# Products over 40 head dims and of 40 output rows, issued with the two head parities in turns

## The chip, the cores and the metric

The kernel runs on one core of a Trainium2 chip. The metric is the device time of one execution in microseconds. TensorE does the products, VectorE (DVE in the profile) and ScalarE (ACT) read its results from PSUM, GpSimd (POOL) does two elementwise products and the indirect DMAs, SyncE issues most DMAs.

## What is computed

Two blocks follow each other, all in float32. The first is a recurrence over 768 time steps for 4 batch rows and 8 heads of 40 dims:

```python
for t in range(S):
    kt, vt, rt = (k[:, :, t], v[:, :, t], r[:, :, t])
    wt, at, bt = (w[:, :, t], a[:, :, t], b[:, :, t])
    y[:, :, t] = np.einsum('bhd,bhde->bhe', rt, state)
    Sa = np.einsum('bhde,bhe->bhd', state, at)
    state_decay = state * wt[:, :, None, :] - np.einsum('bhd,bhe->bhde', Sa, bt)
    state = state_decay + np.einsum('bhd,bhe->bhde', vt, kt)
```

Its output, 3072 rows of 8 x 40 = 320, goes through a layer of 8 experts: each row takes the expert with the largest logit, `relu(x @ w1[e]) @ w2[e]` with 1024 hidden columns, times that expert's softmax weight.

## The kernel before

The first part cuts the time into 6 chunks of 128 steps. A unit `u` is one chunk `c` of one batch row `b`, with all 8 heads: 24 units, the batch rows going fastest. Heads come in pairs: head 2p + par lies at partitions par x 64 to par x 64 + 39 of a tile, for p from 0 to 3 (`rows(par)`); par is the head's parity. A product over the 40 head dims therefore uses rows 0 to 63 of TensorE's array for parity 0 and rows 64 to 127 for parity 1. One with 40 output rows uses one half of its columns in the same way.

For each unit `prepare` forms the running product of the decay, scales the inputs and transposes four of them (`ps_nat`, L169). `systems` builds, for one parity and then the other, four masked products over the 40 dims of both operands, 128 x 128 for each of the four heads: GT, NT0, N and AT (L177, mask on VectorE at L182). From NT0 and N it forms powers: NT1 and the next N, to NT5, each a product of 128 x 128 matrices, copied by ScalarE (L180). `attend` then, parity by parity, forms the right side r (a product with the state, 40 rows, L224, and one with GT, 128 rows, L225, into one bank), and runs X through eight steps (`ps_q`, L216): each is a product of one NT with X and a sum on VectorE (L233, L242), and the next needs that sum. The result u is transposed (`ps_uT`, L246). Then for each parity: ZT, a masked product over 40 dims (L177 again); y, of three products for each head (with the state S, 40 rows, L263; with AT, L264; with ZT, L267); the state's update `ps_s` of 40 output rows (L273, L274), and the transpose of the new state (`ps_st`, L284). `route` transposes the rows of y, forms the logits and stores the rows.

PSUM's eight banks are shared by two kinds of tiles: `big` has five, `small` three, each tile in a bank of its own.

The second part ranks the rows by expert, gathers them and runs the expert layers (L474, L487).

The kernel is written in the order above, with `prepare` and `systems` of the next unit ahead of `attend`, but the instructions of each engine are put in order by a scheduler when the program is built. It moves work of the next unit's `systems` between the dependent steps of X. The order shown below is what it made.

## Time and profile before

| | |
|---|---|
| median of 2 runs | 2519.51 us (2518.1 to 2520.93) |
| profiled execution, first to last instruction | 2515.5 us |
| PE busy | 2373.8 us |
| PEld (weight loads) busy | 2069.5 us |
| DVE, ACT, POOL busy | 529.6, 415.7, 151.8 us |
| mean granted TensorE clock | 0.716 of full speed |

The profiled execution is 4.0 us shorter than the median, for what lies around the instructions. The clock has two levels, full (2.4 GHz, 1.0 in the profile) and half (1.2 GHz, 0.5); a mean between them is a mix of stretches. A float32 product appears as two weight loads (PEld) and two matmuls (PE) for each head; a transpose as one of each. A steady unit stands between 868 and 960 us; most rows below are from it.

### The profile page before, as it was taken

How to read it: one execution, taken by the hardware profiler on the slowest of the kernel's cores; microseconds unless marked ns; L12 is line 12 of the kernel's file. 1: busy time of each engine (PE TensorE's matmuls, PEld its weight loads, DVE VectorE, ACT ScalarE, POOL GpSimd, SP SyncE). 2: the span in 40 equal slices, each digit the busy share in tenths (PEclk: the TensorE clock that was granted, in tenths of full speed). 3: DMA queues.
4: the chain of work that ended last, by engine and by line, in shares of the span. 5: the costliest groups of instructions: out<-in, count | busy, mean ns of one | idle time of the engine just before them, and what ended most of it. 6: DMA issues, size and time to landing. Idle time of an engine off the chain costs nothing.

```text
span 2515.5 us, 29177 instructions
## 1 busy us (share of the span) xinstructions
PE 2373.8 (94%) x12916; PEld 2069.5 (82%) x12916; DVE 529.6 (21%) x1157; ACT 415.7 (17%) x849; POOL 151.8 (6%) x185
## 2 busy tenths in 40 slices
PE   6999999999999999999999999999999998699998
PEld 5999988998898898898899899899889887244544
DVE  2212222122122122122212112213112111311110
ACT  1312211221121121121121121111112110001010
POOL 4000000000000000000000000000000000311101
PEclk9877657766765766666676676676677665799999
DMA  1000000000000000000000000000000000522210
GB/s 48 19 9 11 19 19 16 4 19 19 1 19 19 3 17 19 10 10 19 16 3 19 16 4 19 19 1 19 19 1 19 3 1 3 155 93 85 86 51 16
DMA packets 20560, 59.58 MB, mean 24 GB/s; under 512 B 2893, under 2 KB 14159, under 8 KB 18512
## 3 DMA queue, kind: packets, MB, share of 16 engines
q1 hardware_dynamic: 16992, 48.50, 6.6%
q0 software_dynamic: 3072, 9.18, 1.2%
q8 instruction: 102, 1.67, 0.3%
q14 instruction: 26, 0.21, 0.0%
q10 hardware_dynamic: 368, 0.01, 0.0%
HBM read 49.82 MB, written 9.18 MB: 23 GB/s over the span
## 4 chain that ended last, share of the span: by engine, by line
PE 82%; issue 11%; DVE 3%; POOL 2%; ACT 1%; DMA 0%; POOLq 0%; DVEq 0%; ACTq 0%
PE ps_q L216 20%; PE ps_NT L177 14%; PE ps_N L177 11%; PE ps_y L264 4%; PE ps_ZT L177 4%; PE ps_y L267 4%; PE ps_y L263 3%; PE ps_nat L169 3%; PE ps_r L225 3%; PE ps_r L224 3%; PE ps_AT L177 3%; PE ps_GT L177 3%; DVE X L233 2%; POOL out_dram L493 1%; PE ps_st L284 1%
## 5 line engine op out<-in xcount | busy, mean ns | idle before, releaser
L216 PE MATMUL ps_q<-X,NT 128*128 128x40 f32 x2304 | 399.7, 332 | 52.7 <-DVE X L233 50.2
L216 PEld LDWEIGHTS ps_q<-X,NT 128*128 128x128 f32 x2304 | 378.2, 248 | 70.1 <-DVE X L233 65.7
L177 PE MATMUL ps_NT<-NT,N 128*128 128x128 f32 x1920 | 332.6, 326 | 1.3 <-ACT N L180 1.0
L177 PEld LDWEIGHTS ps_NT<-NT,N 128*128 128x128 f32 x1920 | 282.6, 226 | 13.2 <-issue 8.9
L177 PE MATMUL ps_N<-N,NT 128*128 128x128 f32 x1536 | 249.7, 317 | 0.0
L180 ACT COPY NT<-ps_NT 128x512 f32<-128x512 f32 x240 | 140.4, 585 | 584.9 <-PE ps_NT L177 584.9
L177 PEld LDWEIGHTS ps_N<-N,NT 128*128 128x128 f32 x1536 | 235.2, 234 | 0.0
L233 DVE TENSOR_TENSOR X<-ps_q,X 128x160 f32<-128x160 f32 x240 | 77.6, 323 | 574.9 <-PE ps_q L216 574.9
L474 PE MATMUL hp<-xgT,w 128*128 128x512 f32 (+1 forms) x384 | 190.9, 627 | 0.0
L474 PEld LDWEIGHTS hp<-xgT,w 128*128 128x128 f32 (+1 forms) x384 | 63.2, 189 | 122.4 <-issue 120.4
L216 PE MATMUL ps_q<-Z,NT 128*128 128x40 f32 x768 | 142.1, 348 | 20.5 <-DVE Z L242 20.5
L216 PEld LDWEIGHTS ps_q<-Z,NT 128*128 128x128 f32 x768 | 135.8, 266 | 27.7 <-DVE Z L242 27.7
L487 PE MATMUL zp<-w,h_sb 128*128 128x320 f32 x512 | 145.0, 433 | 0.0
L180 ACT COPY N<-ps_N 128x512 f32<-128x512 f32 x192 | 112.3, 585 | 107.9 <-PE ps_N L177 107.9
L264 PE MATMUL ps_y<-natK,AT 128*128 128x40 f32 x384 | 123.0, 420 | 0.0
L487 PEld LDWEIGHTS zp<-w,h_sb 128*128 128x128 f32 x512 | 94.6, 191 | 34.5 <-issue 0.8
L267 PE MATMUL ps_y<-natB,ZT 128*128 128x40 f32 x384 | 120.1, 415 | 0.0
L267 PEld LDWEIGHTS ps_y<-natB,ZT 128*128 128x128 f32 x384 | 101.9, 327 | 6.8 <-issue 4.3
L264 PEld LDWEIGHTS ps_y<-natK,AT 128*128 128x128 f32 x384 | 96.4, 311 | 13.3 <-issue 0.9
L177 PE MATMUL ps_ZT<-in,uT 40*128 40x128 f32 x384 | 101.0, 440 | 4.6 <-ACT uT L248 2.7
L263 PE MATMUL ps_y<-S,in 40*128 40x40 f32 x320 | 100.9, 414 | 0.0
L158 POOL MEMSET PT<- 128x4 f32 x24 | 2.5, 105 | 1573.8 <-DVE ST L279 1280.2
(150 smaller groups left out, 2384.4 us busy)
## 6 DMA issues: line engine op xcount, KB each, us to landing
in<-in_packed_dram SPq DMA_DIRECT2D x48, 480.0 KB
w<-in_moe_w_dram SPq DMA_DIRECT2D x8, 1280.0 KB
w<-in_moe_w_dram SPq DMA_DIRECT2D x8, 1024.0 KB
x_rows<-xs SPq DMA_DIRECT2D x24, 160.0 KB
w<-in_moe_w_dram SPq DMA_DIRECT2D x8, 256.0 KB
xg<-x_rows,g_idx POOLq DMA_INDIRECT x32
out_dram<-zo,s_idx POOLq DMA_INDIRECT x32
wg_sb<-in_moe_w_gate_dram ACTq DMA_DIRECT2D x2, 4.0 KB
```

The lines of the kernel that those rows point to most:

```text
L169: nc.tensor.transpose(ps[:, p, :], src[:, p, :], ident[:])
L177: nc.tensor.matmul(ps[:, p, :], lhsT=lhs(p), rhs=rhs(p), start=True, stop=True)
L180: nc.scalar.copy(t[:], ps[:])
L216: nc.tensor.matmul(q[:, p, :], lhsT=m[:, p, :], rhs=x[:, p, :], start=True, stop=True)
L224: nc.tensor.matmul(q[:, p, :], lhsT=I[rs, A, p, :], rhs=ST[rs, p, :], start=True, stop=False)
L225: nc.tensor.matmul(q[:, p, :], lhsT=d["GT", par][:, p, :], rhs=nV[:, p, par, :D], start=(c == 0), stop=True,)
L233: nc.vector.tensor_tensor(Xn[:], q[:], X[:], op=ALU.add)
L263: nc.tensor.matmul(q[:, p, :], lhsT=I[rs, R, p, :], rhs=Sn[rs, p, :], start=True, stop=False)
L264: nc.tensor.matmul(q[:, p, :], lhsT=d["AT", par][:, p, :], rhs=nK[:, p, par, :D], start=(c == 0), stop=False,)
L267: nc.tensor.matmul(q[:, p, :], lhsT=ZT[:, p, :], rhs=nB[:, p, par, :D], start=False, stop=True)
L474: nc.tensor.matmul(hp[:, :cols], lhsT=g["w"][0][:dsz, db, fb * 128 : (fb + 1) * 128], rhs=g["xT"][:dsz, db, :cols], start=(db == 0), stop= ...
L487: nc.tensor.matmul(zp[:], lhsT=g["h"][:, fb, j * 128 : (j + 1) * 128], rhs=g["w"][1][:, fb, :], start=(fb == 0), stop=(fb == FB - 1),)
```

## The change

Products over the 40 head dims are issued for both parities together: for each p the product of parity 0 and then that of parity 1, each parity into its own bank. That holds for GT, NT0, N, AT and ZT (the new `product2`), for the products with the state in r and y, and for the new state's transposes. The `ps_s` products share one bank and turn between the two column halves. In r, y and `ps_s` all products with the state (or all of the first kind) come first and those over 128 rows after them, so one bank holds several open sums; only the first product into it starts the bank. All r products now stand ahead of both parities' X steps. `product` keeps the 128-row products alone. Comments and the docstring are taken out. Numbers of products, evacuations and DMAs stay.

```diff
@@ -171,36 +171,48 @@
...
-        def product(lhs, rhs, mask, tag, bufs):
+        def product2(lhs, rhs, mask, tag, bufs):
+
+            pss = [big("ps_" + tag) for _ in range(2)]
+            for p in range(NP):
+                for par in range(2):
+                    nc.tensor.matmul(pss[par][:, p, :], lhsT=lhs(par, p), rhs=rhs(par, p), start=True, stop=True)
+            ts = []
+            for par in range(2):
+                t = sb.tile([128, NP, 128], F32, name=tag, bufs=bufs)
+                nc.vector.tensor_tensor(t[:], pss[par][:], mask[:, None, :].to_broadcast([128, NP, 128]), op=ALU.mult)
+                ts.append(t)
+            return ts
+
+        def product(lhs, rhs, tag, bufs):
             ps = big("ps_" + tag)
             for p in range(NP):
-                nc.tensor.matmul(ps[:, p, :], lhsT=lhs(p), rhs=rhs(p), start=True, stop=True)
+                nc.tensor.matmul(ps[:, p, :], lhsT=lhs[:, p, :], rhs=rhs[:, p, :], start=True, stop=True)
             t = sb.tile([128, NP, 128], F32, name=tag, bufs=bufs)
-            if mask is None:
-                nc.scalar.copy(t[:], ps[:])
-            else:
-                nc.vector.tensor_tensor(t[:], ps[:], mask[:, None, :].to_broadcast([128, NP, 128]), op=ALU.mult)
+            nc.scalar.copy(t[:], ps[:])
             return t
...
+
+            def of(n):
+                return lambda par, p: I[rows(par), n, p, :]
+
+            d["GT"] = product2(of(K), of(A), before, "GT", 4)
+            NT0 = product2(of(B_), of(A), before, "NT0", 4)
+            N0 = product2(of(A), of(B_), after, "N", 4)
+            d["AT"] = product2(of(V), of(R), before, "AT", 4)
+            d["NT"] = []
             for par in range(2):
-                def of(n, par=par):
-                    return lambda p: I[rows(par), n, p, :]
-
-                def mat(t):
-                    return lambda p: t[:, p, :]
-                d["GT", par] = product(of(K), of(A), before, "GT", 4)
-                NTk = product(of(B_), of(A), before, "NT0", 4)
-                Nk = product(of(A), of(B_), after, "N", 4)
-                d["AT", par] = product(of(V), of(R), before, "AT", 4)
-                d["NT", par] = [NTk]
+                NTk, Nk = NT0[par], N0[par]
+                chain = [NTk]
                 for i in range(1, LEVELS + 1):
-                    NTn = product(mat(Nk), mat(NTk), None, f"NT{i}", 4)
+                    NTn = product(Nk, NTk, f"NT{i}", 4)
                     if i < LEVELS:
-                        Nk = product(mat(NTk), mat(Nk), None, "N", 4)
+                        Nk = product(NTk, Nk, "N", 4)
                     NTk = NTn
-                    d["NT", par].append(NTk)
+                    chain.append(NTk)
+                d["NT"].append(chain)
...
@@ -216,25 +228,32 @@
...
+            qs = [small("ps_r") for _ in range(2)]
+            if c:
+                for p in range(NP):
+                    for par in range(2):
+                        nc.tensor.matmul(
+                            qs[par][:, p, :], lhsT=I[rows(par), A, p, :], rhs=ST[rows(par), p, :],
+                            start=(p == 0), stop=False, skip_group_check=True,
+                        )
+            for p in range(NP):
+                for par in range(2):
+                    nc.tensor.matmul(
+                        qs[par][:, p, :], lhsT=d["GT"][par][:, p, :], rhs=nV[:, p, par, :D],
+                        start=(c == 0 and p == 0), stop=True, skip_group_check=True,
+                    )
             for par in range(2):
-                rs = rows(par)
-                q = small("ps_r")
-                for p in range(NP):
-                    if c:
-                        nc.tensor.matmul(q[:, p, :], lhsT=I[rs, A, p, :], rhs=ST[rs, p, :], start=True, stop=False)
-                    nc.tensor.matmul(
-                        q[:, p, :], lhsT=d["GT", par][:, p, :], rhs=nV[:, p, par, :D], start=(c == 0), stop=True,
-                    )
+                q = qs[par]
                 X = sb.tile([C, NP, D], F32, name="X", bufs=6)
                 nc.scalar.copy(X[:], q[:])
                 for i in range(LEVELS):
-                    q = apply(d["NT", par][i], X)
+                    q = apply(d["NT"][par][i], X)
...
@@ -252,26 +271,44 @@
...
+            ZT = product2(lambda par, p: uT[rows(par), p, :], lambda par, p: I[rows(par), R, p, :], before, "ZT", 4)
+            qs = [small("ps_y") for _ in range(2)]
+            if c:
+                for p in range(NP):
+                    for par in range(2):
+                        nc.tensor.matmul(
+                            qs[par][:, p, :], lhsT=I[rows(par), R, p, :], rhs=Sn[rows(par), p, :],
+                            start=(p == 0), stop=False, skip_group_check=True,
+                        )
             for par in range(2):
-                rs = rows(par)
-                ZT = product(
-                    lambda p: uT[rs, p, :], lambda p: I[rs, R, p, :], before, "ZT", 2,
-                )
-                q = small("ps_y")
-                for p in range(NP):
-                    if c:
-                        nc.tensor.matmul(q[:, p, :], lhsT=I[rs, R, p, :], rhs=Sn[rs, p, :], start=True, stop=False)
+                for p in range(NP):
                     nc.tensor.matmul(
-                        q[:, p, :], lhsT=d["AT", par][:, p, :], rhs=nK[:, p, par, :D], start=(c == 0), stop=False,
+                        qs[par][:, p, :], lhsT=d["AT"][par][:, p, :], rhs=nK[:, p, par, :D],
+                        start=(c == 0 and p == 0), stop=False, skip_group_check=True,
                     )
-                    nc.tensor.matmul(q[:, p, :], lhsT=ZT[:, p, :], rhs=nB[:, p, par, :D], start=False, stop=True)
-                nc.vector.tensor_tensor(x[:, :, par, :], q[:], nP[:, :, par, :D], op=ALU.mult)
-
-                if c + 1 < NCH:
-                    q = small("ps_s")
-                    for p in range(NP):
-                        nc.tensor.matmul(q[rs, p, :], lhsT=nK[:, p, par, :D], rhs=nV[:, p, par, :D], start=True, stop=False)
-                        nc.tensor.matmul(q[rs, p, :], lhsT=nB[:, p, par, :D], rhs=U[:, p, par, :D], start=False, stop=True)
+                    nc.tensor.matmul(
+                        qs[par][:, p, :], lhsT=ZT[par][:, p, :], rhs=nB[:, p, par, :D],
+                        start=False, stop=True, skip_group_check=True,
+                    )
+                nc.vector.tensor_tensor(x[:, :, par, :], qs[par][:], nP[:, :, par, :D], op=ALU.mult)
+
+            if c + 1 < NCH:
+
+                q = small("ps_s")
+                for p in range(NP):
+                    for par in range(2):
+                        nc.tensor.matmul(
+                            q[rows(par), p, :], lhsT=nK[:, p, par, :D], rhs=nV[:, p, par, :D],
+                            start=(p == 0), stop=False, skip_group_check=True,
+                        )
+                for p in range(NP):
+                    for par in range(2):
+                        nc.tensor.matmul(
+                            q[rows(par), p, :], lhsT=nB[:, p, par, :D], rhs=U[:, p, par, :D],
+                            start=False, stop=True, skip_group_check=True,
+                        )
...
@@ -279,14 +316,17 @@
...
-                    q = small("ps_st")
-                    for p in range(NP):
-                        nc.tensor.matmul(q[rs, p, :], lhsT=STn[rs, p, :], rhs=ident[rs, rs], start=True, stop=True)
-                    nc.scalar.copy(Snn[rs], q[rs])
+                qs = [small("ps_st") for _ in range(2)]
+                for p in range(NP):
+                    for par in range(2):
+                        rs = rows(par)
+                        nc.tensor.matmul(qs[par][rs, p, :], lhsT=STn[rs, p, :], rhs=ident[rs, rs], start=True, stop=True)
+                for par in range(2):
+                    nc.scalar.copy(Snn[rows(par)], qs[par][rows(par)])
```

The scheduler makes another order from it. Three places, on TensorE, for one unit in the middle of the program; the number at a name's end is the buffer, `x4` says that four instructions (one for each p) follow each other.

First, the start of `systems`. Before, `ps_GT_4972` and the three rows after it are parity 0, `ps_GT_5063` and those after it parity 1, 17 rows later:

```order
L177 MATMUL ps_GT_4972<-in2_131 128x128 x4
L177 MATMUL ps_NT0_4979<-in2_131 128x128 x4
L177 MATMUL ps_N_4986<-in2_131 128x128 x4
L177 MATMUL ps_AT_4993<-in2_131 128x128 x4
L177 MATMUL ps_NT1_5000<-NT0_4984,N_4991 128x128 x4
```

```order
L177 MATMUL ps_GT_5063<-in2_131 128x128 x4
L177 MATMUL ps_NT0_5070<-in2_131 128x128 x4
L177 MATMUL ps_N_5077<-in2_131 128x128 x4
L177 MATMUL ps_AT_5084<-in2_131 128x128 x4
L177 MATMUL ps_NT1_5091<-NT0_5075,N_5082 128x128 x4
```

Now (4962 and 4976 are parity 0, 4963 and 4977 parity 1):

```order
L179 MATMUL ps_GT_4962<-in2_131 128x128
L179 MATMUL ps_GT_4963<-in2_131 128x128
L179 MATMUL ps_GT_4962<-in2_131 128x128
L179 MATMUL ps_GT_4963<-in2_131 128x128
L179 MATMUL ps_NT0_4976<-in2_131 128x128
L179 MATMUL ps_NT0_4977<-in2_131 128x128
```

All 32 products of the two parities now stand in one run, in turns, and the powers of both parities follow them.

Second, y. Before, for one parity, the products over 40 rows (L263) stand between those over 128 rows:

```order
L267 MATMUL ps_y_4839<-natB_4035,ZT_4837 128x40
L263 MATMUL ps_y_4839<-S1_2975,in0_129 128x40
L264 MATMUL ps_y_4839<-natK_4028,AT_4070 128x40
L267 MATMUL ps_y_4839<-natB_4035,ZT_4837 128x40
L263 MATMUL ps_y_4839<-S1_2975,in0_129 128x40
```

Now those over 40 rows come first, in turns and ahead of the transposes of u:

```order
L279 MATMUL ps_y_4837<-S1_2970,in0_129 128x40
L279 MATMUL ps_y_4838<-S1_2970,in0_129 128x40
L265 MATMUL ps_uT_4813<-ident_61,u1_145 128x128 x4
L279 MATMUL ps_y_4838<-S1_2970,in0_129 128x40
L285 MATMUL ps_y_4837<-natK_4020,AT_4088 128x40
L285 MATMUL ps_y_4838<-natK_4020,AT_4090 128x40
L300 MATMUL ps_s_4865<-natV_4013,natK_4020 40x40 x8
L306 MATMUL ps_s_4865<-u1_145,natB_4027 40x40
L179 MATMUL ps_ZT_4823<-in0_129,uT_4818 128x128
L179 MATMUL ps_ZT_4824<-in0_129,uT_4818 128x128
```

Behind the ZT products stand seven more of `ps_s`, then the remaining products of y over 128 rows. The next unit's r follows in runs of one parity, not in turns: four of L235, four of L241 (GT), three of L235, one of L235, four of L241.

Third, the end of the X steps. Before:

```order
L177 MATMUL ps_NT5_5147<-NT4_5138,N_5145 128x128 x4
L216 MATMUL ps_q_5231<-X_5229,NT0_4611 128x40 x4
L216 MATMUL ps_q_5238<-X_5236,NT1_4632 128x40 x4
L216 MATMUL ps_q_5245<-X_5243,NT2_4646 128x40 x4
L216 MATMUL ps_q_5252<-X_5250,NT3_4660 128x40 x4
L216 MATMUL ps_q_5259<-X_5257,NT4_4674 128x40 x4
L216 MATMUL ps_q_5266<-X_5264,NT5_4688 128x40 x4
L216 MATMUL ps_q_5273<-Z_5271,NT5_4688 128x40 x4
L216 MATMUL ps_q_5280<-Z_5278,NT5_4688 128x40 x4
```

Now:

```order
L228 MATMUL ps_q_5221<-X_5219,NT0_4525 128x40 x4
L190 MATMUL ps_NT4_5123<-NT3_5114,N_5121 128x128 x4
L190 MATMUL ps_N_5130<-N_5121,NT3_5114 128x128 x4
L228 MATMUL ps_q_5228<-X_5226,NT1_4623 128x40 x4
L190 MATMUL ps_NT5_5137<-NT4_5128,N_5135 128x128 x4
L228 MATMUL ps_q_5235<-X_5233,NT2_4637 128x40 x4
L228 MATMUL ps_q_5242<-X_5240,NT3_4651 128x40 x4
L228 MATMUL ps_q_5249<-X_5247,NT4_4665 128x40 x4
L228 MATMUL ps_q_5256<-X_5254,NT5_4679 128x40 x4
L228 MATMUL ps_q_5263<-Z_5261,NT5_4679 128x40 x4
L228 MATMUL ps_q_5270<-Z_5268,NT5_4679 128x40 x4
```

The second parity's eight steps start earlier: two of them now stand between products of the powers, six stand alone.

Counted over TensorE's order in the first part: places where one product uses another number of array rows or columns than the one ahead go from 1070 to 469, in a full unit from 51 to 23. Places where a product over 40 dims (64 rows of the array) is followed by one in the other row half go from 4 to 1066; turns between the two column halves from 0 to 280.

## Rows read from the trace of the kernel before

**Rows 1.** The page's first part, and the granted clock in 40 slices of its second.

```profile
PE 2373.8 (94%) x12916; PEld 2069.5 (82%) x12916; DVE 529.6 (21%) x1157; ACT 415.7 (17%) x849; POOL 151.8 (6%) x185
...
PEclk9877657766765766666676676676677665799999
```

**Rows 2.** Stretches: start:end, length, busy by engine, PEclk, DMA share, GB/s.

```profile
868.00:960.20 92.20, 89.09 (x512) 83.40 (x510) 19.85 (x42) 15.97 (x33) 2.55 (x3) 0.65 0.05 13
2142.00:2515.00 373.00, 345.07 (x1020) 168.87 (x1020) 59.59 (x169) 32.71 (x64) 67.54 (x68) 0.96 0.26 81
```

**Rows 3.** The chain of waits: start us, us, what; eight loads a row.

```profile
900.18 2.00 PE ps_GT L177 x8
...
905.59 1.71 PE ps_AT L177 x8
...
921.75 0.89 PE ps_NT L177 x8
```

**Rows 4.** Stretches of the unit at 868 us, columns as in rows 2.

```profile
900.18:907.30 7.12, 7.12 (x33) 6.89 (x33) 2.08 (x3) 0.58 (x1) 0.00 (x0) 0.50 0.06 23
920.67:924.90 4.23, 4.23 (x33) 4.01 (x33) 2.08 (x3) 0.58 (x1) 0.00 (x0) 0.87 0.00 0
911.48:916.93 5.45, 5.45 (x49) 5.45 (x50) 0.65 (x2) 2.34 (x4) 0.00 (x0) 1.00 0.01 3
924.90:934.76 9.86, 9.86 (x50) 9.86 (x50) 1.02 (x2) 2.34 (x4) 0.00 (x0) 0.54 0.01 2
...
942.97:958.25 15.28, 12.29 (x65) 11.27 (x64) 2.27 (x7) 0.58 (x1) 0.00 (x0) 0.65 0.00 1
868.11:897.58 29.47, 29.35 (x140) 26.23 (x141) 8.60 (x15) 2.65 (x8) 2.55 (x3) 0.50 0.13 34
```

**Rows 5.** The chain of waits in y and r; two loads a row.

```profile
874.74 0.58 PE ps_y L263 x2
875.31 0.58 PE ps_y L264 x2
875.89 0.43 PE ps_y L267 x2
...
889.98 0.58 PE ps_r L224 x2
...
937.44 0.34 PE ps_r L224 x2
```

**Rows 6.** The chain of waits, ZT of both parities.

```profile
869.83 2.08 PE ps_ZT L177 x8
...
872.59 1.57 PE ps_ZT L177 x6
...
879.48 0.72 PE ps_ZT L177 x2
```

**Rows 7.** The timeline of weight loads at 1885 us: start, us, what, idle before.

```profile
1885.29 2.80 PEld L177 LDWEIGHTS ps_ZT<-in,uT 40*128 40x128 f32 x16 [1.07 <-ACT uT L248]
```

**Rows 8.** Stretches, ZT instructions alone: length, busy PE, PEld, DVE, then PEclk.

```profile
961.90:963.95 2.05, 2.01 (x8) 1.78 (x8) 0.00 (x0) 0.50 0.00 0
...
1885.87:1886.30 0.43, 0.43 (x4) 0.43 (x3) 0.00 (x0) 0.50 0.00 0
1886.30:1886.73 0.43, 0.43 (x6) 0.43 (x6) 0.00 (x0) 0.50 0.00 0
```

**Rows 9.** The chain of waits, two steps of X next to each other.

```profile
951.63 1.94 PE ps_q L216 x8
...
953.97 1.94 PE ps_q L216 x8
```

**Rows 10.** Groups by line on DVE: out, in, count, busy us, mean ns, idle before.

```profile
L161 DVE RECIPROCAL in<-PT 128x512 f32<-128x512 f32 x24 | 80.5, 3352 | 0.8
...
L160 DVE TENSOR_TENSOR_SCAN PT<-in,zeros_c 128x128 f32<-128x128 f32 x96 | 35.1, 409 | 17.0 <-DMA in<-in_packed_dram 15.3
...
L182 DVE TENSOR_TENSOR GT<-ps_GT,before 128x512 f32<-128x512 f32 x48 | 33.2, 692 | 117.0 <-PE ps_GT L177 116.9
```

More of the change, by code (lines that the diff above doesn't have):

```diff
@@ L236, in attend @@
                 for i in range(3):
-                    q = apply(d["NT", par][LEVELS], X)
+                    q = apply(d["NT"][par][LEVELS], X)
                     if i < 2:
@@ L281, in attend @@
                         nc.vector.tensor_tensor(STn[rs], q[rs], PC, op=ALU.mult)
-                    q = small("ps_st")
-                    for p in range(NP):
-                        nc.tensor.matmul(q[rs, p, :], lhsT=STn[rs, p, :], rhs=ident[rs, rs], start=True, stop=True)
-                    nc.scalar.copy(Snn[rs], q[rs])
+                qs = [small("ps_st") for _ in range(2)]
+                for p in range(NP):
+                    for par in range(2):
+                        rs = rows(par)
+                        nc.tensor.matmul(qs[par][rs, p, :], lhsT=STn[rs, p, :], rhs=ident[rs, rs], start=True, stop=True)
+                for par in range(2):
+                    nc.scalar.copy(Snn[rows(par)], qs[par][rows(par)])
             return x
```

## The prediction, made before the changed kernel ran

> **What bounds the kernel.** The page's first and second parts come first [rows 1]: TensorE is busy 94% of the span and its weight loads 82%, while the granted clock stands at 0.5 to 0.8 of full from the second slice to the 35th. The table by stretches then parts the program: a steady unit of the first part takes 92.2 us at a mean clock of 0.65, and the experts take 373 us at 0.96 [rows 2]. The change touches no line of the experts, so these 373 us stay. The chain of waits inside one unit is TensorE almost throughout; the pieces below are read from there.
>
> Three prices follow.
>
> *Weight loads.* Every float32 product is two loads and two matmuls. Eight loads of 128 columns follow each other in 1.71 us at half clock (0.2135 each) and in 0.89 us at full clock (0.111) [rows 3], whether 40 or 128 rows are used: a 40-row product costs what a 128-row one costs.
>
> *Changes of tile.* 40-row operands use half of the array's rows. In the y products each step of 64-row and 128-row tiles shows the cost of going from one to the other: two loads right after a change take 0.58, two without one 0.43 [rows 5]. I take 0.15 us a change at half clock; where the moving side has 128 columns it is 0.29 (2.00 against 1.71 for eight, [rows 3]).
>
> *Two row halves.* In four places of the trace before, all in the last units, the ZT products of one head parity are directly followed by those of the other, in the other half of the rows and another bank. There 16 loads take 2.80 us [rows 7], though eight alone take 1.78 [rows 8], and 16 in one line would need 1.78 + 8 x 0.2135 = 3.49. The cells of 0.43 us show how: three loads touch a cell before the meeting and six at it [rows 8]. The halves work at the same time, each at its own 0.2135. Only some four products on each side meet there; the change makes all of them meet.
>
> **The change, by one full unit.** Each piece is set against the rows of the unit at 868 us.
>
> 1. *GT, NT0, N, AT.* Before: 7.12 + 4.23 = 11.35 us, the first parity at half clock, the second mostly at full [rows 4]. After, the order has all 64 loads in one run, parities in turns. As two lines that is 32 x 0.2135 + 0.29 = 7.1 at half clock. Gain 4.2. Bounds: without any overlap 64 x 0.2135 + 0.29 = 13.95, a loss of 2.6; at full clock VectorE's eight evacuations of 0.692 [rows 10] set at least 5.5, a gain of 5.8. I take half clock, since the stretch ahead of it is at 0.50 [rows 4]. There a pair of products takes 1.71 and its two evacuations 1.38, so VectorE keeps up.
>
> 2. *ZT.* Before 2.08 + 1.57 + 0.72 = 4.37 [rows 6]; after 8 x 0.2135 + 0.37 (the 2.08 less eight loads) = 2.1. Gain 2.3; without overlap 0.6.
>
> 3. *y.* Before, eight times 0.58 + 0.58 + 0.43 = 12.7 [rows 5]. After, 32 loads of 128 rows (6.8), 16 of 64 rows in two lines (1.7), and four changes, since one of the S products lands behind the transposes of u (0.6): 9.1. Gain 3.6; without overlap 1.9.
>
> 4. *r.* Before, eight pieces of 0.58 at half clock and eight of 0.34 at full [rows 5]: 7.4. After, the order has not turned them: four of a parity, then four with GT, and the second parity now comes before the products too, at half clock. 32 loads are 6.8 and six changes 0.9: 7.7. Loss 0.3.
>
> 5. *The clock.* The clock is 1.00 over the six groups at 911.48, falls inside the second parity's products (0.87 on average), and the six groups after them take 9.86 us at 0.54, against 5.45 for the six before [rows 4]. TensorE never paused: it was busy 4.23 of 4.23 us. What differs from the stretches that held full clock is that for these 32 loads only half the array's rows were used. After the change there is no second run of products in the middle, and the one at the start fills both halves. So these six groups run at 5.45: gain 4.4. Bounds: nothing, if the clock falls for another reason; or 1.6 more, if the fuller products raise the clock earlier and two more groups run in 0.89 in place of 1.71 [rows 3].
>
> 6. *The tail of X.* Before, eight groups of q stand at the unit's end with nothing between, 15.28 us [rows 4], each waiting for the sum of the group ahead. With r done early, the order now has two of them between the last N and NT groups; six remain. A group in the tail at half clock is 2.34 us from the next [rows 9], a group between others 5.45 / 6 = 0.91. Gain 2 x 1.43 = 2.9.
>
> Changes of tile in a full unit fall from 51 to 23 by the order. Those outside y, r and ZT change by few, and I take nothing for them. State products (ps_s) in turns use two halves of the columns; no row shows whether these overlap. Their price stays between the present 0.13 for two loads and half of it, under 1.1 us a unit, and I take none.
>
> *What it delays.* Both parities' y now wait for both ZT, so ZT's second evacuation (0.69) stands ahead of the state's sums on VectorE; TensorE has seven state products there (0.9 us) and then the first parity's y. VectorE's scans and the 3.35 us reciprocal [rows 10] for the next unit follow y, and the transposes of K wait for them; between y and these transposes the order has two state transposes, all of r and a group of q, some 11 us against 3.35 + 4 x 0.41 for the scans. If that cover went, the excess would show ahead of K. The second parity's r keeps one of three small banks until its copy; two are left for q, which uses them in turns. No DMA is added or moved past another on SP or POOL. For waits of this kind that I don't see I take off 1 us a unit.
>
> *Sum.* 4.2 + 2.3 + 3.6 - 0.3 + 4.4 + 2.9 = 17.1 a full unit, and 16 of 24 units are full (a state before and after): 274. The first four have no S products and spend less at half clock: ZT, the tail and about 3 of the rest, 8 each, 32. The last four: three with 14, one without a next unit, 6: 48. Together 354, less 24 for waits: 330. The profiled span is 2515.5 and the median of the runs 2519.5, 4 us around the span, which stay: 2519.5 - 330 = about **2190 us**.
>
> **Rivals.**
>
> *A, the clock doesn't follow.* If the fall at 924 us has another cause, piece 5 is gone in some 20 units: 2190 + 88 = 2280. For it: the rise and fall are seen, their cause is inferred from which products stood ahead. Against it: the two falls of this unit come at the half-filled products and in the tail, the two kinds of work that use the array least. The Trainium skill (TensorE: Matmul & The Clock Gate, "HAM oscillation — how this bites in real kernels") puts falls of the clock down to gaps in TensorE's work. The busy 4.23 of 4.23 us does not agree with that; by this rule the change could not move the clock and the time would be A's.
>
> *B, no overlap in strict turns.* The meetings in the trace are between runs of four; single turns may not overlap. Then pieces 1 to 3 lose 6.8 + 1.7 + 1.7 = 10.2 a unit, over 22 units 225: about 2415, still faster through fewer changes, the clock and the tail. Against it: at the meetings, loads of both parities alternate in time already.
>
> *C, full clock earlier.* Fuller products raise the clock during piece 1: 1.4 + 1.6 a unit more, over 20 units 60: 2130. VectorE's 0.692 a product is then the floor, 1.38 against 0.89 for a pair. The Trainium skill (TensorEngine Tiling (Array Packing), "Performance Considerations") says that tiling speeds up TensorE and not the emptying of PSUM; rows 10 agree, and by it C gains no more than this.
>
> *D, slower.* Going from one row half to the other costs like a change of tile, in each of the 1066 places that the order has. At 0.15 to 0.29 each, 0.2 in the middle, 213 us on top of B: about 2630. It decides from 0.10 us a turn (B's 105 us of gain over 1066). Against it: at the four meetings the next load starts within the same cell, with no pause.
>
> That the change doesn't do what it says holds only for r, which the order leaves unturned; that is counted.
>
> **The numbers.** Forecast 0.58, A 0.15, C 0.12, B 0.10, D 0.05. The likeliest is 2190. The range takes in the forecast with its bounds, A and C, and leaves out B and D: 2090 to 2330. A measurement of this kernel can tell about 2% (50 us) from no change. Forecast, A, B and C are all beyond that: faster 0.93; same 0.02 for a case between B and D; slower 0.05.
>
> **What would show it.** Right: 16 loads of GT in some 1.8 to 2.0 us at half clock; one run of products a unit and no half-clock stretch between it and the tail; six q groups in the tail; units of about 75 to 78 us; the experts still 373. Wrong: 16 loads of a pair in 3.4 us or more (B, D); a fall to half clock among the NT and N groups (A); idle TensorE ahead of y, of the transposes of K or among the products, released by VectorE.

## The result, and the profile after

The changed kernel takes 2145.87 us (median of 2 runs, 2145.71 to 2146.03) against 2519.51: a ratio of 0.8495, with a 95% interval of 0.8404 to 0.8586. It is faster by 373.6 us; 330 were predicted (2190, range 2090 to 2330). The profiled execution's span is 2144.2 us (2515.5 before), its mean clock 0.756 (0.716).

The page of the changed kernel, the lines that answer to [rows 1]:

```profile
PE 2009.8 (94%) x12916; PEld 1751.6 (82%) x12916; DVE 511.5 (24%) x1157; ACT 417.3 (19%) x849; POOL 151.1 (7%) x185
...
PEclk9987668756766786678667657866777657999999
```

TensorE is still the bound, with the same number of instructions and the same 94%; it is busy 364 us less. A steady unit, by stretches, answering to [rows 2] (columns as there):

```profile
1148.00:1224.00 76.00, 73.82 (x520) 70.34 (x520) 19.17 (x42) 16.77 (x35) 2.54 (x3) 0.69 0.06 16
```

The chain of waits of the same unit (start us, us, what). It answers to [rows 3, 5, 6]: there, two loads of `ps_y` took 0.58, 0.58 and 0.43 in turn, two of `ps_r` 0.58 at half clock, and ZT took 2.08, 1.57 and 0.72.

```profile
1171.53 1.86 PE ps_y L279 x14
1173.38 1.04 PE ps_uT L265 x4
1174.43 0.58 PE ps_y L279 x2
1175.01 1.00 PE ps_y L285 x4
1176.01 0.69 PE ps_s L300 x16
1176.70 0.12 PE ps_s L306 x2
1176.83 2.06 PE ps_ZT L179 x16
1178.89 0.68 DVE ZT L183
...
1189.17 1.86 PE ps_r L235 x8
1191.03 1.86 PE ps_r L241 x8
1192.88 1.43 PE ps_r L235 x6
...
1194.89 0.58 PE ps_r L235 x2
1195.47 1.86 PE ps_r L241 x8
...
1202.31 2.01 PE ps_GT L179 x16
1204.32 1.71 PE ps_NT L179 x16
1206.02 1.71 PE ps_N L179 x16
1207.73 1.71 PE ps_AT L179 x16
```

What to see: 16 loads of both parities now take what eight loads of one parity took. GT is 2.01 for 16 (2.00 for eight in [rows 3]), AT 1.71 (1.71 for eight). The clock's stretches of this unit and the next:

```profile
1211.80:1239.10 27.30, 26.47 (x231) 26.10 (x229) 3.57 (x11) 10.42 (x19) 0.00 (x0) 1.00 0.00 1
...
1239.10:1286.90 47.80, 46.46 (x284) 43.35 (x283) 15.60 (x31) 5.84 (x15) 2.54 (x3) 0.50 0.09 25
```

There is one stretch at full clock, over the powers and the first q groups of the tail, and one at half clock over the rest. The second half-clock stretch of the kernel before, 924.90 to 934.76 in [rows 4], is gone.

Where the 371.3 us of the span went, cut at the first transposes of u of units 3, 19 and 23:

| stretch | before | after | less | predicted |
|---|---|---|---|---|
| start to unit 3's u | 330.8 | 294.5 | 36.2 | 32 |
| 16 full units | 1460.0 | 1179.9 | 280.1 | 274 |
| last four | 326.8 | 275.3 | 51.5 | 48 |
| behind the last u, with the experts | 397.9 | 394.5 | 3.4 | 0 |
| waits taken off | | | 0 | -24 |

### The profile page after: what moved, and what is told of

Same layout as the page of the kernel before. It is cut to its first block, busy times and chain, and to the rows that moved or that the text cites. A ratio compares the mean times of both kernels' runs of the same rounds, so it can differ in the third digit from the quotient of the medians.

```text
span 2144.2 us, 29192 instructions
## 1 busy us (share of the span) xinstructions
PE 2009.8 (94%) x12916; PEld 1751.6 (82%) x12916; DVE 511.5 (24%) x1157; ACT 417.3 (19%) x849; POOL 151.1 (7%) x185
## 4 chain that ended last, share of the span: by engine, by line
PE 75%; issue 13%; DVE 4%; POOL 2%; DMA 0%; ACT 0%; POOLq 0%; DVEq 0%; ACTq 0%
PE ps_q L228 20%; PE ps_NT L190 11%; PE ps_N L190 8%; PE ps_y L289 4%; PE ps_y L285 4%; PE ps_r L241 4%; PE ps_nat L169 4%; PE ps_r L235 3%; PE ps_y L279 2%; PE ps_ZT L179 2%; PE ps_GT L179 2%; PE ps_AT L179 1%; POOL out_dram L533 1%; PE ps_N L179 1%; DVE X L252 1%
## 5 line engine op out<-in xcount | busy, mean ns | idle before, releaser
L228 PE MATMUL ps_q<-X,NT 128*128 128x40 f32 x2304 | 352.8, 308 | 36.2 <-DVE X L252 36.2
L228 PEld LDWEIGHTS ps_q<-X,NT 128*128 128x128 f32 x2304 | 334.6, 223 | 48.2 <-DVE X L252 47.3
L190 PE MATMUL ps_NT<-NT,N 128*128 128x128 f32 x1920 | 286.5, 297 | 3.9 <-DVE N L183 2.7
L190 PEld LDWEIGHTS ps_NT<-NT,N 128*128 128x128 f32 x1920 | 244.6, 201 | 12.1 <-DVE N L183 5.1
L190 PE MATMUL ps_N<-N,NT 128*128 128x128 f32 x1536 | 212.1, 283 | 0.0
L190 PEld LDWEIGHTS ps_N<-N,NT 128*128 128x128 f32 x1536 | 197.2, 201 | 0.0
L228 PEld LDWEIGHTS ps_q<-Z,NT 128*128 128x128 f32 x768 | 132.2, 260 | 28.7 <-DVE Z L261 28.0
L285 PE MATMUL ps_y<-natK,AT 128*128 128x40 f32 x384 | 115.6, 414 | 0.0
L169 PE MATMUL ps_nat<-ident,in 128*128 128x128 f32 x288 | 71.6, 417 | 24.7 <-DMA in<-in_packed_dram 16.7
L261 DVE TENSOR_TENSOR Z<-ps_q,X 128x160 f32<-128x160 f32 x96 | 31.2, 325 | 225.1 <-PE ps_q L228 225.1
```

What stands on the lines that cost most here:

```text
L169: nc.tensor.transpose(ps[:, p, :], src[:, p, :], ident[:])
L190: nc.tensor.matmul(ps[:, p, :], lhsT=lhs[:, p, :], rhs=rhs[:, p, :], start=True, stop=True)
L228: nc.tensor.matmul(q[:, p, :], lhsT=m[:, p, :], rhs=x[:, p, :], start=True, stop=True)
L285: nc.tensor.matmul(qs[par][:, p, :], lhsT=d["AT"][par][:, p, :], rhs=nK[:, p, par, :D], start=(c == 0 and p == 0), stop=False, skip_group_ ...
```

## The experiments

The kernel before ran beside each group of them and took 2525 to 2527 us there. Ratios are to it. The changed kernel did not run again beside them, and the interval of its ratio (0.8404 to 0.8586) is some 23 us to either side: a run nearer to its 2146 us than that is not told from it by its time, only by its trace.

### Products alone

The kernel before, with `product2` for GT, NT0, N, AT and ZT; r, y and the state as before:

```diff
-                d["GT", par] = product(of(K), of(A), before, "GT", 4)
+            GT = product2(of(K), of(A), before, "GT", 4)
```

> The kernel before (2519.5 us) with the five masked products in turns at the start of the unit, and r, y, state and tail as before (47 changes of tile a unit, eight groups of q in the tail). Theory: pieces 1, 2 and 5 of the sum, 4.2 + 2.3 + 4.4 = 10.9 a unit over some 22 units, 240 us: about 2280. If the clock does not follow the products (rival A), pieces 1 and 2 alone, 6.5 a unit: about 2375.

Measured: 2287.55 us, ratio 0.9047 (0.8992 to 0.9102). The theory's case, far from the 2375 of rival A. 238 us over 22 units are 10.8 each; pieces 1, 2 and 5 were 4.2 + 2.3 + 4.4 = 10.9. Only the mean agrees, though. Two units of the trace, between the transposes of u:

```profile
1027.00:1105.10 78.10, 74.94 (x511) 69.28 (x510) 19.07 (x42) 16.00 (x33) 2.55 (x3) 0.72 0.06 16
...
1183.20:1268.70 85.50, 82.39 (x511) 76.82 (x509) 19.35 (x42) 16.00 (x33) 2.55 (x3) 0.64 0.05 14
```

In the first the clock rises as its products begin (1058.4 us), and it gains 14 us on the 92.1 of before. The second has them at half clock and gains 6.6, about what pieces 1 and 2 are without the clock (6.5): its powers have no second fall, but the clock rises only 8.5 us into them (2.8 in the kernel before, 910.1 against 907.30). That the mix of such units comes to 10.8 is in part luck.

### Sums alone

The changed kernel, with GT, NT0, N and AT issued where they stood before, one parity ahead of the first powers and the other between the powers; ZT, r, y and the state stay in turns:

```diff
-            d["GT"] = product2(of(K), of(A), before, "GT", 4)
+            for par in range(2):
+                d["GT"].append(half(par, of(K), of(A), before, "GT"))
```

> The changed kernel with GT, NT0, N and AT of each parity where they stood before, those of parity 1 behind parity 0's powers; ZT, r, y and the state as changed (25 changes of tile a unit, six groups of q in the tail). Theory: ZT 2.3, y 3.0, state 1.0, tail 2.7 less r 0.2: 8.8 a unit over 22 units, 195 us: about 2325, with a fall of the clock inside the unit as before. Rival, the clock's gain comes with the r products' place and not with the masked products: 4.4 a unit more, about 2230, and one stretch of full clock a unit.

Measured: 2353.93 us, ratio 0.9338 (0.9297 to 0.9379): 29 us above the theory's figure and far from the rival. In the trace the 16 full units are 8.6 us shorter each, near the 8.8 expected. What is missing comes from the units at the start: the program reaches the u of unit 3 at 336.9 us, where the kernel before does at 330.8; why was not looked into. The clock still falls inside the unit. Two stretches of one, and what TensorE did in them:

```profile
785.70:795.90 10.20, 10.20 (x90) 10.05 (x90) 2.36 (x5) 3.71 (x7) 0.00 (x0) 1.00 0.00 0
795.90:806.10 10.20, 10.20 (x50) 9.97 (x49) 1.71 (x3) 1.76 (x3) 0.00 (x0) 0.50 0.01 2
```

The second parity's GT begins at 793.03, and the clock falls where the last of its four masked products, AT, begins (795.90), with TensorE busy all the time. With both parities' products in one run there is no such fall among the powers.

### Runs of four

`product2` with its two loops exchanged: four products of one parity, then four of the other, for each matrix.

```diff
-                for p in range(NP):
-                    for par in range(2):
+                for par in range(2):
+                    for p in range(NP):
```

> The changed kernel (2146 us) with the five masked products issued as four of one parity and then four of the other, in place of single turns. Turns needed (theory): two runs of four overlap only where they meet, 0.73 us a meeting at half clock (the 3.49 less 2.80 of the ZT rows before). Products 13.95 - 7 x 0.73 = 8.8 against 7.1, ZT 3.05 against 2.06: 2.7 us a unit more. The order now happens to put r in turns: 1.7 for 16 loads that overlap and 0.5 for fewer changes of tile less. Net +0.5 a unit: about 2158 us. Rival 1, any neighbouring halves overlap in full however they stand: -2.2 a unit, about 2095. Rival 2, no overlap without single turns: +6.3 a unit, about 2290.

Measured: 2159.26 us, ratio 0.8559 (0.8517 to 0.8601), near the theory's 2158, in part by luck, and by its time not told from the changed kernel. The chain of waits at a place where the parity changes:

```profile
766.77 2.38 PE ps_GT L179 x13
769.15 0.17 PE ps_NT L179
...
771.19 0.17 PE ps_N L179
```

From one meeting to the next 16 loads take 2.04 us (769.15 to 771.19), in place of 1.71: the halves overlap in part only. All 64 loads, with the ends that meet nothing, take 9.1 us in place of 7.1, and ZT 3.02 in place of 2.06. That is 3 us a unit, where 2.7 were expected: a meeting saves 3.49 - 2.80 = 0.69, and not the 0.73 put down there, and with 0.69 the products come to the measured 9.1. The total rose by 13 us only, and in the trace the 16 full units take as long as in the changed kernel (1179.5 against 1179.9). In this order the scheduler put r's products with the state in turns, which gives a part back (see four small banks), and ten of the 16 units have the full clock from about their products on and are of 71.1 to 71.2 us, where the changed kernel has five such units, of 70.4. So it is the chain at the meetings that speaks against rivals 1 and 2, more than the total.

### Parity by parity

The four masked products of parity 0 and then those of parity 1, at the same place of the order as in the changed kernel:

```diff
-            d["GT"] = product2(of(K), of(A), before, "GT", 4)
+            for par in range(2):
+                d["GT"].append(half(par, of(K), of(A), before, "GT"))
+                NT0.append(half(par, of(B_), of(A), before, "NT0"))
```

> The changed kernel with GT, NT0, N and AT of parity 0 and then those of parity 1, still all at the start of the unit; the rest of TensorE's order is that of the changed kernel, to the row. Overlap is what products gain (theory): one meeting is left, 13.95 - 0.73 = 13.2 us against 7.1, 6.1 a unit more over 23 units, 140 us; and the half-filled run keeps the clock down, so units that begin their products at full clock go too, some 20 us: about 2290 to 2305. Rival, the gain came from moving the second run out of the middle and from fewer changes of tile, and not from overlap: 2146.

Measured: 2291.25 us, ratio 0.9074 (0.9035 to 0.9114): the theory's case. One change of the parity in this run of products in place of 31 costs 145 us. The pieces differ from the theory's, so its figure was in part luck: most units begin their products at full clock, and the run takes 10.2 us and not 13.2. The stretches of a unit, its products from 768.54 to 778.73:

```profile
768.50:771.90 3.40, 3.40 (x32) 3.40 (x33) 1.82 (x3) 0.59 (x1) 0.00 (x0) 1.00 0.13 48
771.90:782.10 10.20, 10.20 (x52) 9.98 (x51) 3.71 (x6) 0.59 (x1) 0.00 (x0) 0.50 0.01 2
782.20:809.50 27.30, 26.10 (x226) 25.61 (x224) 3.90 (x12) 10.16 (x18) 0.00 (x0) 1.00 0.00 1
```

Here the half-filled run takes the full clock away within the run itself. TensorE is busy 3.40 of 3.40 us, then 10.20 of 10.20 at half clock. The Trainium skill (TensorE: Matmul & The Clock Gate, "HAM oscillation — how this bites in real kernels") puts falls down to gaps in TensorE's work; these rows have none, so here the measurement decides.

### The second run on 128 rows

The kernel before, in its old order, with parity 1's masked products formed from all 128 partitions:

```diff
-                    return lambda p: I[rows(par), n, p, :]
+                    return lambda p: I[rows(par) if par == 0 else slice(0, 128), n, p, :]
```

> The kernel before, with one edit: GT, NT0, N and AT of parity 1 are formed from all 128 partitions instead of rows 64 to 103, so their values are the sums over both parities. The order of the work and the number of loads are the same; only the filled rows of the array in the second run of products differ. Theory (a run of products on half the rows takes the clock away): the clock stays at 1.00 through that run and the six groups behind it; the run takes 32 x 0.111 + evacuation, about 4.2 us, and the six groups 5.45 instead of 9.86. 4.4 to 4.8 us a unit over some 18 units: about 2435 us. Rival (the fall has another cause, a pause or the time since the rise): the clock falls where it fell, 2519 us.

Measured: 2459.53 us, ratio 0.9731 (0.9687 to 0.9775). Stretches of one unit: the second run of products, the groups behind it, and where the clock then falls.

```profile
810.19:813.76 3.57, 3.57 (x32) 3.38 (x31) 2.08 (x3) 0.58 (x1) 0.00 (x0) 1.00 0.00 0
813.76:822.22 8.46, 8.41 (x74) 8.33 (x73) 1.34 (x3) 3.51 (x6) 0.00 (x0) 1.00 0.01 2
824.50:827.90 3.40, 3.40 (x18) 3.24 (x16) 0.00 (x0) 1.17 (x2) 0.00 (x0) 0.50 0.00 0
```

The full clock now survives the run, which was at 0.87 in [rows 4], and the groups behind it, of which the first six were at 0.54. Only the filled rows differ, and with them the values, which were not parted from the rows. So what fills the array in that run decides that fall. The gain is 68 us and not 84; in a unit like this one a shorter fall (3.4 us at half clock, 10.2 before) comes later, behind r's first products, which have 40 columns and in part 40 rows.

### The state's sums by parity

The `ps_s` products parity by parity, so that the two column halves stand behind each other:

```diff
-                for p in range(NP):
-                    for par in range(2):
+                for par in range(2):
+                    for p in range(NP):
```

> The changed kernel with the ps_s products issued parity by parity instead of in turns (all else in the same order). Theory (the two column halves work at the same time when they are issued in turns): the 16 loads of the first kind, 0.69 us in the changed kernel, take 16 x 0.067 = 1.07 us; 0.4 to 0.8 us a unit over 20 units: 2154 to 2162 us. Rival (the columns do not overlap and 0.69 has another cause, such as a mixed clock): 0.69 again and 2146 us.

Measured: 2164.18 us, ratio 0.8566 (0.8530 to 0.8601), 18 us above the change, which its time alone does not show, and 2 us above the theory's range. The weight loads on the timeline (start, us, what) of this run and then of the changed kernel:

```profile
1109.92 0.77 PEld L300 LDWEIGHTS ps_s<-natV,natK 128*40 128x40 f32 x14
...
1112.91 0.77 PEld L306 LDWEIGHTS ps_s<-u,natB 128*40 128x40 f32 x14 [0.22 <-issue]
```

```profile
1175.94 0.62 PEld L300 LDWEIGHTS ps_s<-natV,natK 128*40 128x40 f32 x16
...
1178.77 0.61 PEld L306 LDWEIGHTS ps_s<-u,natB 128*40 128x40 f32 x14 [0.22 <-issue]
```

Column halves in turns overlap as well: 14 loads in 0.61 against 0.77, 16 in 0.62. The Trainium skill (TensorEngine Tiling (Array Packing), "Key Properties") says that different tiles can load and multiply in parallel; the rows agree, for row and for column halves. The loads side with the theory and against the rival, by 0.16 us for 14 of them, less than expected. Most of the 18 us are not these tenths, though, so that the total came near the theory's is luck. Twelve of the 16 full units of this run are of 75.1 us, while in the changed kernel five of 16 are of 70.4, with full clock from the products on, and two of 77.8. That the short units are gone is seen; whether so small a shift did it, and how, is open.

### Four small banks

PSUM as four big and four small banks; the order then has r's products with the state in turns:

```diff
-            return pp.tile([128, NP, 128], F32, name=name, tag="big", bufs=5)
+            return pp.tile([128, NP, 128], F32, name=name, tag="big", bufs=4)
-            return pp.tile([128, NP, D], F32, name=name, tag="small", bufs=3)
+            return pp.tile([128, NP, D], F32, name=name, tag="small", bufs=4)
```

> The changed kernel with PSUM's banks shared as four big and four small instead of five and three. The order then issues r's products with the state in turns (20 changes of tile a unit instead of 23). Theory (in the changed kernel r's 40-row products were not in turns, and turns would save what they saved elsewhere): in the run in runs of four, where r stands in turns, its 16 loads with the state take 1.00 + 1.43 = 2.43 us instead of about 3.9; 1.4 us a unit over 20 units: about 2118 us. Rival (one bank less for the products: the third pair waits for VectorE's first evacuations, 1.38 a pair against 1.71 of loads at half clock but against 0.89 at full): no loss in units at half clock, 1 to 1.5 us more in the ten units whose products run at full clock: 2130 to 2146 us.

Measured: 2112.08 us, ratio 0.8359 (0.8341 to 0.8377). The chain of waits in a unit with full clock at its products:

```profile
821.19 1.86 PE ps_r L235 x16
...
832.09 1.37 PE ps_GT L179 x16
833.46 1.28 DVE GT L183 x2
```

Both mechanisms are there. r's 16 loads take 1.86 us, where the changed kernel's chain has 1.86 + 1.43 + 0.58 = 3.87. And with one bank less TensorE waits 1.28 us for VectorE's two evacuations when the clock is full. Nine of the 16 full units have the full clock from about their products on and are of 69.0 to 69.1 us, where the changed kernel has five such units, of 70.4. So the 34 us that are left are not the turns of r alone.

### The kernel before with wide q

X in tiles of 128 columns, 88 of them zeros, so that a product of the tail moves 128 columns:

```diff
-                q = small("ps_q")
+                q = pp.tile([128, NP, 128], F32, name="ps_q", tag="small", bufs=3)
-                    Xn = sb.tile([C, NP, D], F32, name="X", bufs=6)
-                    nc.vector.tensor_tensor(Xn[:], q[:], X[:], op=ALU.add)
+                    Xn = wide()
+                    nc.vector.tensor_tensor(Xn[:, :, :D], q[:, :, :D], X[:, :, :D], op=ALU.add)
```

> The kernel before, with X in tiles of 128 columns (40 of X, 88 of zeros), so that the q products move 128 columns; the rest of the order is nearly the same. Theory (the narrow products of the tail take the clock): its eight groups take 8 x 1.57 = 12.6 us instead of 15.3 and the first part of the state stage runs at full clock too; the fall inside the second parity's products stays, since they fill half of the rows; 10 to 12 us a unit over 22 units: 2255 to 2300 us, and the change's turns are then still worth 350 to 400 us beside the wide q. Rival 1 (once the clock is held, the turns are worth what they save in loads at full clock, 9 to 12 us a unit): 2100 to 2165 us. Rival 2 (in the kernel before the clock is lost in the half-filled and mixed stages whatever the tail does): only the tail's 2 to 3 us a unit, about 2460 us.

Measured: 2298.73 us, ratio 0.9117 (0.9075 to 0.9158), the theory's upper end. One unit: the stretch with the second run of products, and the fall that stays inside it.

```profile
905.90:919.50 13.60, 13.60 (x119) 13.40 (x118) 2.70 (x7) 4.68 (x8) 0.00 (x0) 1.00 0.00 1
919.50:926.30 6.80, 6.80 (x33) 6.58 (x33) 1.37 (x3) 1.17 (x2) 0.00 (x0) 0.50 0.00 0
```

### The change with wide q

The same edit on the changed kernel.

> The changed kernel with X kept in tiles of 128 columns (40 of X, 88 of zeros), so that the q products move 128 columns instead of 40; loads, sums and their number stay, 88 columns a product are added. Theory (how much of the array works, not whether TensorE pauses alone, decides the clock): the tail of X keeps full clock, and part of the state stage behind it; the q groups cost 0.89 instead of 0.89 between others (loads set the pace) and 1.5 to 2 in the tail as now; 3 to 5 us a unit less: about 2050 us. Rival 1 (the dependent tail's pauses take the clock whatever the products' width): each tail group grows by the longer drain, some 0.1 to 0.3 us, 24 x 7 x 0.15: about 2170 us. Rival 2 (nothing changes): 2146 us.

Measured: 1903.72 us, ratio 0.7533 (0.7500 to 0.7565). The direction is the theory's, but the time is 146 us below its figure: I had left the state stage at half clock. Most of it runs at full clock too, until just ahead of r, and a unit is of 62 to 64 us in place of 74.9. The stretches: one unit's full and half clock, and the next tail.

```profile
855.80:903.60 47.80, 44.91 (x441) 42.28 (x437) 12.75 (x31) 11.82 (x22) 0.00 (x0) 1.00 0.06 17
903.60:917.20 13.60, 13.60 (x65) 12.79 (x64) 6.14 (x12) 2.67 (x10) 2.56 (x3) 0.50 0.11 23
946.43:956.77 10.34, 7.84 (x59) 6.58 (x57) 1.95 (x6) 0.59 (x1) 0.00 (x0) 1.00 0.01 2
```

The same place in the changed kernel:

```profile
1236.36:1246.44 10.08, 8.04 (x42) 7.40 (x42) 1.62 (x5) 0.00 (x0) 0.00 (x0) 0.64 0.01 2
```

Both tails pause for VectorE behind each group, and TensorE idles 2.5 us of 10.3 in the one and 2.0 of 10.1 in the other. The one with wide products keeps 1.00, the narrow one is at 0.64. So the pauses alone do not take the clock here: the width of the q products makes the difference. All of them are wide in this run, among the powers too, and which of them keep the clock in the tail was not parted. Against the kernel before with wide q the change is worth 395 us here: its gain does not shrink when more of the clock is kept (a mean of 0.821 there and 0.894 here).

This version beats both kernels: 242 us below the changed one.

### Wide r and y

As the last one, with the 128-row products of r and y over 128 columns (both parities' inputs, of which the own 40 are used):

```diff
-                        qs[par][:, p, :], lhsT=d["GT"][par][:, p, :], rhs=nV[:, p, par, :D],
+                        qs[par][:, p, :, :], lhsT=d["GT"][par][:, p, :], rhs=nV[:, p, :, :],
```

> As the run with q over 128 columns, and the 128-row products of r and y also move 128 columns (both parities' inputs, of which only the own parity's 40 are used). Loads stay the same in number; r stands later in the order and eleven q groups are left in the tail instead of six. Theory (work of the array sets the clock): the state stage and the tail run near full clock, 25 to 30 us of half clock a unit become 13 to 17; less about 5 for the five groups more in the tail: 1850 to 1950 us. Rival (the clock is lost in the tail and the state stage by their pauses and 40-row products): five more groups alone, 5 x 1.0 us x 20 units more: about 2250 us.

Measured: 1927.48 us, ratio 0.7633 (0.7595 to 0.7671): in the theory's range, yet above the run with wide q alone. The mean clock rises from 0.894 to 0.930, but the scheduler's new order takes more than that back. The tail has eleven groups in place of seven, and a wait that the former run had for 1.7 us in all, of `ps_xT` for y's evacuation, is now 61.6 (what waited, for what: us, times, longest):

```profile
PE ps_xT L346 <- DVE x L303: 61.6, 23, 3.3
```

The chain of waits of one unit shows what stood ahead of that evacuation on VectorE, the next unit's reciprocal:

```profile
805.06 3.35 DVE in L170
808.41 0.19 DVE x L303
```

This is one of the waits that the prediction looked for in the changed kernel; it came here.

### Wide q and r, four small banks

> The run with q over 128 columns, with four big and four small banks (r's products with the state in turns) and r's 128-row products over 128 columns too; the tail keeps its seven groups. In that run the one half-clock stretch of a unit, some 14 to 17 us, held r (7.6 us), the first q group and the transposes of K. Theory (narrow products ahead of it take the clock): r in turns and wide keeps full clock: half of the 14 to 17 us and 1 us of r, 6 to 8 us a unit over 20 units: 1745 to 1785 us. Rival (the clock is gone before r because of y's 40-column products, and the stretch only moves): 1 to 1.5 us a unit for the turns: about 1875 us.

The edits are those of four small banks and, in r alone, of wide r and y. Measured: 1937.89 us, ratio 0.7673 (0.7657 to 0.7689). Both figures failed; the rival's mechanism is the nearer. r itself fell from 7.6 to some 6 us, but steady units are of 57.5 to 64.6 us, all but one with 10 to 20 us at half clock, which in the unit below begins at ZT already. Its chain of waits:

```profile
922.18 1.78 PE ps_ZT L188 x16
...
934.24 1.86 PE ps_r L244 x16
...
944.50 1.14 PE ps_GT L188 x16
945.64 1.28 DVE GT L192 x2
```

ZT's 1.78 is mostly at half clock, where the run with five big banks has 1.14. The 1.28 us for VectorE is the price of the bank, now paid with the clock full. The first three units also got slower, 67.8, 68.0 and 62.9 us against 60.1, 58.5 and 58.5; what holds those up was not looked into. How much of the loss is the bank's and how much the wide r's was not parted.

## Why the prediction was right, and which terms were mis-sized

Point by point, one full unit of before [rows 4 to 6, 9] against the unit of the chain above (1173.38 to the next u at 1248.30, 74.9 us; 92.1 before):

| piece | predicted | measured |
|---|---|---|
| 1 products | +4.2 | 11.35 to 7.13: +4.2 |
| 2 ZT | +2.3 | 4.37 to 2.06: +2.3 |
| 3 y | +3.6 | 12.7 to 9.6: +3.1 |
| 4 r | -0.3 | 7.4 to 7.6: -0.2 |
| 5 clock: the powers without r and the second run | +4.4 | 28.7 to 24.4: +4.3 |
| 6 tail of X | +2.9 | 15.3 to 10.9, less 1.7 for the two groups moved: +2.6 |
| state's sums | 0 | 2.04 to 0.81 on the chain: +1.2 |
| wait for u's copy, for ZT | -1 with all waits | +0.66 and -0.72 |

The piece 5 is the time from the first power to the tail: before 907.30 to 942.97 less 4.23 for the second run and 2.76 for r, after 1209.44 to 1235.50 less the two groups of q. The sum is 17.4, and the units differ by 17.2. The table's last two rows belong together: 14 of the state's 32 loads (0.61 us, the row at 1178.77 above) now stand inside the 0.72 that y waits for ZT. All 32 took 2.04 and now take 0.69 + 0.12 + 0.61 = 1.42, so the turns are worth 0.6, and of the 0.72 TensorE's loads stand still for about 0.2.

*Products and ZT.* The rate of the four meetings holds for strict turns. Rival B would have had 3.4 us and more for 16 loads, the trace has 1.71; and rival D's price of a turn would show as more than that. Runs of four show what was left between. Both rivals fall.

*Clock.* The fall inside the second run is gone. The mechanism, half-filled rows and not a pause, was inferred from one place; parity by parity brings the fall back, and the run on 128 rows takes it away without moving anything. Rival A falls. The size of the piece also hangs on how early the clock rises among the powers: 2.4 us into them in this unit, 8.5 in the second unit shown of products alone, where the powers gained 1.7 in place of 4.4 and the tail lost 1.2. What sets that is open.

*Rival C* came true in a part: in the five units of 70.4 us the products stand at full clock. The stretch of one, all 64 loads and VectorE's evacuations beside them:

```profile
983.37:987.70 4.33, 4.29 (x66) 3.94 (x65) 3.14 (x6) 0.69 (x2) 0.00 (x0) 1.00 0.10 38
```

They take 4.3 us. The floor of 5.5 that I set from eight evacuations was wrong: five banks let the powers begin before the last ones are emptied. The emptying itself hardly changed: 1.28 us a pair on VectorE, where two of [rows 10] are 1.38.

*The waits*, the mis-sized term. I took 1 us a unit, 24 us, off for waits that I didn't see. The trace's waits on TensorE:

```profile
PE ps_q L228 <- DVE X L252: 36.2, 86, 0.5
PE ps_q L228 <- DVE Z L261: 21.4, 51, 0.5
...
PE ps_y L289 <- DVE ZT L183: 7.9, 8, 3.4
...
PE ps_NT L190 <- DVE N L183: 2.7, 1, 2.7
```

The new ones, for ZT and N, are 10.6 us. The waits for X and Z are 57.6, down from 70.7 (50.2 and 20.5), and the wait for u's copy, 0.66 a unit on the chain at 869 us, is now covered by y and the state's sums: I had not priced that. The reciprocal and scans never showed. So the term should have been about nothing; it is 24 of the 43.6 us by which the time was lower than predicted. The rest is 6.1 in the full units, 7.7 in the first and last, 3.4 in the experts' part, and 2.3 of the runs' medians. Inside the full units, the state's sums were the other unpriced gain, half of it by the turns and half because the rest of them stands in the wait for ZT. I kept them at nothing for lack of a row, although the row halves had shown what halves do.

*Luck.* That the 16 full units come so near, 280.1 for 274, is in part luck: I had all of them alike, while five of 70.4 us give 22 more than at 74.9 each, and two of 77.8 and one of 80.8 take 12 back.

## What to carry to other kernels

Where a product uses half of the array's rows or columns, issue the two halves product by product in turns, not in runs: in turns all of the loads overlap, in runs only those at the meeting. Then look at the clock by stretches, and at what TensorE's products filled just ahead of each fall, not only at its pauses: here runs of products on 40 rows took the clock while TensorE was busy, and zeros that fill 40 columns up to 128 were worth more than the work that they add. Look at the order that the scheduler makes after each edit: here wider products of r and y moved work into the tail and behind VectorE, and the whole took longer than without them.

## What was not expected of the hardware

The zero columns: 88 useless columns in each product of X took 242 us off the changed kernel (2145.9 to 1903.7) and 227 off the kernel before (2526.0 to 2298.7). At full clock a group of eight loads pays little for them: 0.89 instead of 0.82 us between other products, 1.17 instead of 1.10 in the tail.

Two column halves of 40 outputs overlap as well when they are issued in turns: 16 loads take 0.62 us, against 0.77 for 14 issued by parity.

In the run with the state's sums by parity, whose steady unit is 0.2 us longer, the alternation of 74.9, 70.4 and 77.8 us is gone and 12 of 16 units are of 75.1. That the shift did it is not shown; but with a clock that falls and rises within each unit, small terms did not simply add here.
